# One step of a rational activation: its constant is added on ScalarE and its multiply done on GpSimd for all batches, not for the first alone

## The chip, the cores and the metric

The kernel runs on one core of a Trainium2 chip. The core has TensorE (PE, matrix products), VectorE (DVE), ScalarE (ACT), GpSimd (POOL) and SyncE (SP, which issues the DMAs). The metric is the device time of one execution in microseconds.

## The reference

Attention with a threshold feeds two expert layers, one after the other. There are 4 batches, 8 heads, 576 positions and a head size of 64; the model width is 512 and the hidden width 2048.

```python
scores = scale * q @ k.T
thresh = max(scores) - tau
scores = where(scores >= thresh, scores, -1e9)
attn = exp(scores - max(scores)); attn = attn / (sum(attn) + 1e-9)
x = attn @ v                                  # rows x 512

h = x @ w_in                                  # first expert
P = a[0] + a[1]*h + a[2]*h*h + a[3]*h*h*h
Q = 1.0 + abs(b[0])*abs(h) + abs(b[1])*h*h
x = (P / (Q + 1e-6)) @ w_out

h = x @ w2_in                                 # second expert
g = where(h >= 1, h, where(h <= -1, 0, (h + 1)**2 / 4))
out = g @ w2_out
```

The change is in how `P / (Q + 1e-6)` is worked out.

## The kernel before, in words

Every matrix product of the experts is made of three products of 16-bit halves: a tensor is split into a high half (a cast on ScalarE, L203) and the rest (a subtraction on GpSimd, L207).

The experts are worked through in 192 steps: for each batch, first the first expert (m = 0), then the second (m = 1); for each of these, three blocks j of 192 positions; for each block, eight chunks i of 256 hidden units. A step is one `first_product`: 24 matmuls (L838) into a PSUM bank `ph` (two banks, taken in turn), the activation, and the split of its result into `gg` (four buffers). The `second_product` of a step (24 matmuls, L852, into the accumulator `acc`) is issued three steps later (`LAG = 3`), behind the first product of that later step. At the end of a block `end_moe1` copies `acc` to `y` (ScalarE, L795), takes its largest value (VectorE, L797; over all partitions with a matmul and L183) and splits it (L209, L210).

The activation of the first expert is `rational`. On ScalarE: u = |h| (L719), s = the upper part of the polynomial (L720). On VectorE: u becomes the denominator without its constant (L721), and s the polynomial (L722, L723, both read the PSUM bank). ScalarE estimates 1/Q with Ln and Exp (L724, L725) into r. VectorE finishes the numerator times the estimate (L726). Then comes one Newton step: u = (u + constant) * r, and the result (u - 2) * s (L732). The first half of the Newton step has two forms, chosen by `first`: in batch 0 ScalarE adds the constant (L728) and GpSimd multiplies by r (L729); in batches 1 to 3 one VectorE instruction does both (L731). u and r are the halves of one buffer (tag `tp`, 5 buffers), s has the tag `poly` (3 buffers). The second expert's `quadratic` has one ScalarE and two VectorE instructions (L783 to L785).

The attention of batch 0 comes first, with the preparation of the first expert's weights; the second expert's weights are prepared beside steps 0 to 20 (the casts to words of L223 to L225, the splits of L207). The attention of batches 1, 2 and 3 is spread over steps 18 to 50, 60 to 100 and 108 to 147. A row of it: scores on TensorE (L373, L374), a copy with the maximum on VectorE (L419), the threshold's constants (L420, L421), the exponential on ScalarE (L380), the mask on VectorE (L381), the split (ScalarE L389, GpSimd L390 and L392), a transposing DMA (`eT<-hl`) and the product with v (L407). Before the rows, v and the pairs of q and k are scaled and split (L210, L296, L303, L328).

The order of the instructions on each engine isn't written out by hand. The program gives each step and each attention unit a place (`at(...)`), and a planner that simulates the engines with its own costs (`schedule_with_timeline_sim`) orders each engine's queue by these places and by what it expects to be ready. The queues then run in order on the chip.

Of the kernel before, what the change touches and what calls it, by code (L numbers as in the profile page):

```python
# [12 lines left out]
AF = mybir.ActivationFunctionType  # L13
ALU = mybir.AluOpType
# [25 lines left out]
def tile_attention_moe_moe2(  # L40
# [18 lines left out]
    V, A, G, T, Q = nc.vector, nc.scalar, nc.gpsimd, nc.tensor, nc.sync  # L59
# [43 lines left out]
    def small(n, name, keep=False):  # L103
        if keep:
            return cp.tile([P, n], F32, name=name)
        tag = "".join(x for x in name if x.isalpha() or x == "_").rstrip("_")
        return sp.tile([P, n], F32, name=name, tag=f"s{n}_{tag}", bufs=4 if tag in ("mx", "nt") else 2)
# [30 lines left out]
    qc, pc = small(2, "qc", True), small(4, "pc", True)  # L138
# [61 lines left out]
    def split(hi, lo, src, scale=None, on_vector=True):  # L200

        if scale is None:
            A.copy(hi, src)  # L203

            n = E // 4 if tuple(src.shape) == (P, E) else None
            for p in [slice(c, c + n) for c in range(0, E, n)] if n else [slice(None)]:
                G.tensor_tensor(lo[:, p], src[:, p], hi[:, p], op=ALU.subtract)  # L207
        elif on_vector:
            A.activation(hi, src, AF.Copy, scale=scale)  # L209
            V.scalar_tensor_tensor(lo, src, scale, hi, op0=ALU.mult, op1=ALU.subtract)  # L210
        else:
            A.activation(src, src, AF.Copy, scale=scale)  # L212
            split(hi, lo, src)
# [492 lines left out]
    def temp(name):  # L706

        t = mp.tile([P, 2, W], F32, name=name, tag="tp", bufs=N_TEMP)
        return t[:, 0], t[:, 1]

    def rational(ph, i, consts, name, first):

        sc, ka = consts[0], consts[1][:, i, :]
        p = ph.rearrange("p f t -> p (f t)")
        u, r = temp("t0" + name)
        s = mp.tile([P, W], F32, name="t1" + name, tag="poly", bufs=N_POLY)
        A.activation(u, p, AF.Abs, scale=sc[:, i : i + 1])  # L719
        A.activation(s, p, AF.Identity, bias=ka[:, 2:3], scale=ka[:, 3:4])  # L720
        V.scalar_tensor_tensor(u, u, qc[:, 0:1], u, op0=ALU.add, op1=ALU.mult)  # L721
        V.tensor_tensor(s, s, p, op=ALU.mult)  # L722
        V.scalar_tensor_tensor(s, s, ka[:, 1:2], p, op0=ALU.add, op1=ALU.mult)  # L723
        A.activation(r, u, AF.Ln, bias=lc[:, 1:2], scale=lc[:, 0:1])  # L724
        A.activation(r, r, AF.Exp, bias=lc[:, 2:3], scale=-1.0)  # L725
        V.scalar_tensor_tensor(s, s, ka[:, 0:1], r, op0=ALU.add, op1=ALU.mult)  # L726
        if first:
            A.activation(u, u, AF.Identity, bias=qc[:, 1:2])  # L728
            G.tensor_tensor(u, u, r, op=ALU.mult)  # L729
        else:  # L730
            V.scalar_tensor_tensor(u, u, qc[:, 1:2], r, op0=ALU.add, op1=ALU.mult)  # L731
        V.scalar_tensor_tensor(u, u, 2.0, s, op0=ALU.subtract, op1=ALU.mult)  # L732
        return u

# [42 lines left out]
    def quadratic(ph, i, consts, name):  # L777


        top, bias, su, sg, _ = (x[:, i : i + 1] if e < 4 else x for e, x in enumerate(consts))  # L780
        p = ph.rearrange("p f t -> p (f t)")
        u, g = temp("t2" + name)
        A.activation(u, p, AF.Relu, bias=bias, scale=su)  # L783
        V.scalar_tensor_tensor(u, u, top, u, op0=ALU.min, op1=ALU.mult)  # L784
        V.scalar_tensor_tensor(g, p, sg, u, op0=ALU.mult, op1=ALU.max)  # L785
        return g
# [39 lines left out]
    def first_product(m, b, j, i, consts):  # L826
        name = f"{m}_{b}_{j}_{i}"
        w = chunks[m, i][:, 0:HALF].rearrange("p (x kt f) -> p x kt f", x=2, kt=KT)
        ph = ps_1.tile([P, 512], F32, name="ph" + name, tag=f"ph{i % 2}")[:, 0:W].rearrange("p (f t) -> p f t", f=NF)
        for f in range(NF):  # L830
            n = 0
            for kt in range(KT):
                for wx, xx in ((0, 0), (0, 1), (1, 0)):
                    if m == 0:
                        rhs = xT[b][j][:, xx * KT + kt, :]
                    else:
                        rhs = yT[b, j][:, xx * KT + kt, :]
                    last = T.matmul(ph[:, f, :], w[:, wx, kt, f * P : (f + 1) * P], rhs, start=(n == 0), stop=(n == 3 * KT - 1))  # L838
                    n += 1
        g = rational(ph, i, consts, name, b == 0) if m == 0 else quadratic(ph, i, consts, name)  # L840
        gg = mp.tile([P, 2, NF, TB], F16, name="gg" + name, tag="gg", bufs=N_GG)
        hi, lo = (gg[:, x].rearrange("p f t -> p (f t)") for x in range(2))
        split(hi, lo, g)
        return gg, last.ins
# [19 lines left out]
    for n in range(N_FIRST):  # L864
        with at(36 * n / N_FIRST - 40):
            next(att)
        while halves and len(halves) * N_FIRST > 2 * NCH * (N_FIRST - 1 - n):
            with at(2.4 * (2 * NCH - len(halves)) - 40):
                i, x = halves.pop(0)
# [14 lines left out]
    pending, consts, accs, atts = [], {}, {}, {}  # L884
# [14 lines left out]
    for st, (n, m, b, j, i) in enumerate(steps):  # L899
        with at(st):  # L900
            if i == 0:
                if m == 0:
                    consts[m, b, j] = moe1_consts(b) if j == 0 else consts[m, b, 0]
                else:
                    if b == 0 and j == 0:
                        moe2_weights()
                    consts[m, b, j] = moe2_consts(b, j)
            gg, last = first_product(m, b, j, i, consts[m, b, j])
        pending.append((n, m, b, j, i, gg, last))
        if len(pending) > LAG:  # L910
            with at(st + 1.5):
                finish_step()
        for t, u in beside[st]:
            if u[0] == "w":
                with at(t - 3):
                    stage_half(1, u[1], u[2], False)
            else:
                if u[1] not in atts:
                    atts[u[1]] = attention(u[1])
                with at(t - 1.5):  # L920
                    next(atts[u[1]])
# [31 lines left out]
```

## Time and profile before

| | |
|---|---|
| median of 3 runs | 1272.82 us (1270.37, 1272.82, 1278.93) |
| the profiled execution | 1280.63 us, its span 1278.9 us |
| TensorE busy | 1080.8 us, 85% of the span |
| VectorE busy | 1015.8 us, 79% |
| ScalarE busy | 832.4 us, 65% |
| GpSimd busy | 537.6 us, 42% |

The span goes from the first to the last instruction of the profiled execution. A busy share is the mean over the whole span; the stages differ. Steps of the first expert run in about 214 to 357 us (batch 0), 531 to 655 us (batch 1), 795 to 915 us (batch 2) and 1066 to 1168 us (batch 3). Engines overlap, so busy times don't add up to the span.

### The profile page before, as it was taken

The numbers are of one execution on the slowest core, as the hardware profiler recorded it, in microseconds if no ns is written. First come the engines' busy times: TensorE is split into PE (matmuls) and PEld (weight loads), VectorE is DVE, ScalarE is ACT, GpSimd is POOL, SyncE is SP. The second block draws the span as 40 slices with busy tenths as digits, with TensorE's granted clock in tenths as the row PEclk, the third lists the DMA queues.
The fourth block names the chain that finished last, engine by engine and source line by source line (L and its number), as shares of the span: only waits on it lengthen the run. The fifth ranks groups of instructions, "written<-read, shape, count | busy, mean of one in ns | idle before, by whom it ended". The sixth has DMA issues, their size and how long they took to land.

```text
span 1278.9 us, 31212 instructions
## 1 busy us (share of the span) xinstructions
PE 1080.8 (85%) x12354; PEld 973.4 (76%) x12354; DVE 1015.8 (79%) x2379; ACT 832.4 (65%) x1501; POOL 537.6 (42%) x700
## 2 busy tenths in 40 slices
PE   2667874777837999899889999998898998999998
PEld 1344543767737888899788898997798887999997
DVE  6877879899979987779999666889997767897421
ACT  3656676877865776667776566776765666775332
POOL 3314243877744765421355454212454553222221
PEclk9888987888968999999999999999999999999999
DMA  7745446323665766923398448522783568106100
GB/s 212 236 142 178 148 164 215 116 100 123 228 252 156 130 121 122 251 105 88 72 235 177 92 86 207 172 52 55 185 214 65 106 138 226 39 2 231 35 14 26
DMA packets 220340, 176.37 MB, mean 138 GB/s; under 512 B 182048, under 2 KB 193312, under 8 KB 212000
## 3 DMA queue, kind: packets, MB, share of 16 engines
q1 hardware_dynamic: 220192, 174.36, 50.9%
q8 instruction: 97, 1.59, 0.5%
q14 instruction: 51, 0.42, 0.1%
HBM read 106.83 MB, written 21.50 MB: 100 GB/s over the span
## 4 chain that ended last, share of the span: by engine, by line
PE 35%; DVE 26%; DMA 12%; ACT 9%; issue 8%; POOL 7%; SPq 2%; DVEq 0%; POOLq 0%; ACTq 0%
PE ph L838 14%; PE acc L852 14%; DMA eT<-hl 7%; POOL hl L392 3%; DMA qkT<-qk 2%; PE pv L407 2%; DVE e L381 2%; DMA rqk<-in_k_dram 2%; DVE wt L224 2%; DVE sc L419 2%; DVE t L726 2%; ACT wt L212 1%; POOL wh L207 1%; DVE wt L225 1%; POOL wc L207 1%
## 5 line engine op out<-in xcount | busy, mean ns | idle before, releaser
L852 PE MATMUL acc<-gg,wc 128*128 128x192 f16 x4608 | 434.3, 249 | 28.3 <-POOL gg L207 12.7
L838 PEld LDWEIGHTS <-wc 128*128 128x128 f16 x4608 | 392.2, 100 | 45.3 <-issue 20.4
L852 PEld LDWEIGHTS <-wc 128*128 128x128 f16 x4608 | 389.0, 99 | 25.7 <-issue 19.8
L207 POOL TENSOR_TENSOR gg<-t,gg 128x384 f16<-128x384 f32 x192 | 191.0, 996 | 380.3 <-ACT gg L203 312.9
L838 PE MATMUL ph<-xT,wc 128*128 128x192 f16 x2304 | 219.8, 253 | 28.3 <-DVE t L723 13.8
L838 PE MATMUL ph<-yT,wc 128*128 128x192 f16 x2304 | 219.8, 249 | 1.8 <-DVE t L723 1.4
L392 POOL TENSOR_TENSOR hl<-e,hl 128x256 f16<-128x256 f32 x216 | 156.6, 745 | 0.0
L203 ACT CAST gg<-t 128x384 f16<-128x384 f32 x192 | 97.2, 508 | 82.9 <-DVE t L785 41.0
L784 DVE SCALAR_TENSOR_TENSOR t<-t,c 128x384 f32<-128x384 f32 x96 | 66.3, 691 | 69.5 <-ACT t L783 69.1
L381 DVE SCALAR_TENSOR_TENSOR e<-sc,nt,e 128x576 f32<-128x576 f32 x108 | 96.9, 897 | 28.6 <-ACT e L380 28.1
L390 POOL TENSOR_TENSOR hl<-e,hl 128x64 f16<-128x64 f32 x108 | 41.5, 384 | 149.0 <-ACT hl L389 147.9
L380 ACT ACTIVATE e<-sc,nt,con 128x576 f32<-128x576 f32 x108 | 93.5, 866 | 11.5 <-POOL hl L392 4.9
L407 PE MATMUL pv<-v,eT 128*128 128x65 f16 (+3 forms) x1680 | 70.9, 196 | 33.0 <-DMA eT<-hl 31.5
L783 ACT ACTIVATE t<-ph,c 128x384 f32<-128x384 f32 x96 | 63.8, 666 | 50.8 <-PE ph L838 46.3
L389 ACT CAST hl<-e 128x576 f16<-128x576 f32 x108 | 72.0, 668 | 36.8 <-DVE e L381 34.7
L407 PEld LDWEIGHTS <-eT 128*128 128x128 f16 (+1 forms) x1680 | 64.0, 102 | 41.4 <-DMA eT<-hl 38.8
L719 ACT ACTIVATE t<-ph,sc 128x384 f32<-128x384 f32 x96 | 55.3, 576 | 61.1 <-PE ph L838 60.7
L419 DVE TENSOR_SCALAR_CACHE_REDUCE sc<-s 128x576 f32<-128x576 f32 x108 | 80.8, 749 | 13.2 <-PE s L374 12.5
L207 POOL TENSOR_TENSOR wc<-wt,wc 128x256 f16<-128x256 f32 x64 | 52.1, 847 | 79.6 <-ACT wc L203 79.6
L726 DVE SCALAR_TENSOR_TENSOR t<-t,ka,t 128x384 f32<-128x384 f32 x96 | 68.9, 717 | 14.4 <-ACT t L725 14.2
L724 ACT ACTIVATE t<-t,lc 128x384 f32<-128x384 f32 x96 | 67.8, 707 | 14.7 <-DVE t L721 14.3
L373 PE MATMUL s<-qkT 128*128 128x512 f16 (+1 forms) x240 | 63.8, 294 | 14.3 <-DVE sc L419 7.1
(231 smaller groups left out, 1867.8 us busy)
## 6 DMA issues: line engine op xcount, KB each, us to landing
wc<-scratch SPq DMA_DIRECT2D x56, 1024.0 KB, 5.8
rw<-in_moe_w_in_dram SPq DMA_DIRECT2D x16, 1024.0 KB, 5.3
rw<-in_moe_w_out_dram SPq DMA_DIRECT2D x16, 1024.0 KB, 4.9
scratch<-wc SPq DMA_DIRECT2D x8, 1024.0 KB, 4.3
scratch<-wh SPq DMA_DIRECT2D x16, 512.0 KB, 3.3
rqk<-in_q_dram SPq DMA_DIRECT2D x16, 256.0 KB, 3.0
rqk<-in_k_dram SPq DMA_DIRECT2D x16, 256.0 KB, 3.0
kT<-qkT SPq DMA_DIRECT2D x28, 144.0 KB, 2.4
```

Of the source, the lines that this page charges most:

```text
L203: A.copy(hi, src)
L207: G.tensor_tensor(lo[:, p], src[:, p], hi[:, p], op=ALU.subtract)
L380: A.activation(e, s, AF.Exp, bias=nb, scale=con[:, 0:1])
L381: V.scalar_tensor_tensor(e, s, th, e, op0=ALU.is_ge, op1=ALU.mult)
L389: A.copy(hi, e)
L392: G.tensor_tensor(lo_w[:, p], e[:, whole][:, p], hi[:, whole][:, p], op=ALU.subtract)
L407: T.matmul(pv[rows, 0:w], eT[:, c, cols], vv[:, h * NT + x if x < NT else H * NT + h, at : at + w], start=(n == 0), stop=(n == len(blocks) ...
L419: V.tensor_scalar(s, banks[:, 0:S], 1.0, -LARGEST, op0=ALU.mult, op1=ALU.max, accum_out=mx)
L724: A.activation(r, u, AF.Ln, bias=lc[:, 1:2], scale=lc[:, 0:1])
L726: V.scalar_tensor_tensor(s, s, ka[:, 0:1], r, op0=ALU.add, op1=ALU.mult)
L838: last = T.matmul(ph[:, f, :], w[:, wx, kt, f * P : (f + 1) * P], rhs, start=(n == 0), stop=(n == 3 * KT - 1))
L852: T.matmul(dst, w[:, wx, f, d * P : (d + 1) * P], gg[:, gx, f, :], start=(i == 0 and f == 0 and n == 0 and d % 2 == 0), stop=(i == NCH - 1 ...
```

## The change

The argument `first` of `rational` goes, and with it the second form: in all four batches ScalarE adds the constant and GpSimd multiplies by the estimate. The 72 steps of batches 1 to 3 lose one VectorE instruction each and gain one on ScalarE and one on GpSimd; batch 0 has the same instructions as before.

```diff
-    def rational(ph, i, consts, name, first):
+    def rational(ph, i, consts, name):
...
         V.scalar_tensor_tensor(s, s, ka[:, 0:1], r, op0=ALU.add, op1=ALU.mult)
-        if first:
-            A.activation(u, u, AF.Identity, bias=qc[:, 1:2])
-            G.tensor_tensor(u, u, r, op=ALU.mult)
-        else:
-            V.scalar_tensor_tensor(u, u, qc[:, 1:2], r, op0=ALU.add, op1=ALU.mult)
+        A.activation(u, u, AF.Identity, bias=qc[:, 1:2])
+        G.tensor_tensor(u, u, r, op=ALU.mult)
         V.scalar_tensor_tensor(u, u, 2.0, s, op0=ALU.subtract, op1=ALU.mult)
...
-        g = rational(ph, i, consts, name, b == 0) if m == 0 else quadratic(ph, i, consts, name)
+        g = rational(ph, i, consts, name) if m == 0 else quadratic(ph, i, consts, name)
```

## Rows read from the trace of the kernel before

**Rows 1.** The page's busy times: us, share of the span, instructions.
```profile
PE 1080.8 (85%) x12354; PEld 973.4 (76%) x12354; DVE 1015.8 (79%) x2379; ACT 832.4 (65%) x1501; POOL 537.6 (42%) x700
```

**Rows 2.** Busy by stretch: PE, PEld, DVE, ACT, POOL; clock, DMA share, GB/s.
```profile
214.00:357.00 143.00, 112.70 (x1172) 107.14 (x1172) 130.99 (x219) 111.91 (x193) 98.22 (x88) 0.91 0.46 156
575.00:655.00 80.00, 70.08 (x808) 65.45 (x806) 78.99 (x196) 59.67 (x107) 23.94 (x31) 0.98 0.44 113
840.00:915.00 75.00, 64.16 (x738) 59.76 (x737) 72.37 (x182) 54.46 (x98) 21.54 (x27) 0.98 0.39 97
1066.00:1168.00 102.00, 99.52 (x1231) 98.51 (x1229) 91.61 (x201) 74.62 (x138) 24.88 (x29) 1.00 0.28 90
```

**Rows 3.** TensorE's waits, 575 to 655 us: us in total, times, longest.
```profile
PE ph L838 <- DVE t L723: 3.7, 4, 1.8
...
PE acc L852 <- POOL gg L207: 0.2, 1, 0.2
```

**Rows 4.** TensorE's waits, 840 to 915 us.
```profile
PE s L373 <- DVE sc L419: 4.6, 2, 3.0
PE ph L838 <- DVE t L723: 3.3, 3, 2.1
```

**Rows 5.** Timeline of one step: start us, us, instruction, idle before and its releaser.
```profile
562.70 0.62 DVE L726 SCALAR_TENSOR_TENSOR t<-t,ka,t 128x384 f32<-128x384 f32 x1 [0.45 <-ACT t L725]
563.23 0.61 DVE L731 SCALAR_TENSOR_TENSOR t<-t,qc 128x384 f32<-128x384 f32 x1
...
563.83 0.58 ACT L719 ACTIVATE t<-ph,sc 128x384 f32<-128x384 f32 x1 [1.17 <-PE ph L838]
563.88 0.56 DVE L732 SCALAR_TENSOR_TENSOR t<-t,t 128x384 f32<-128x384 f32 x1
...
565.50 0.92 POOL L207 TENSOR_TENSOR gg<-t,gg 128x384 f16<-128x384 f32 x1 [3.04 <-ACT gg L203]
...
571.49 2.15 PE L852 MATMUL acc<-gg,wc 128*128 128x192 f16 x24
```

**Rows 6.** The Newton step's lines: ns min/median/max, first and last start.
```profile
L728 ACT ACTIVATE t<-t,qc x24: 598/602/627, 219.3 to 352.5; 128x384 f32<-128x384 f32 x24
...
L729 POOL TENSOR_TENSOR t<-t x24: 997/1313/2127, 219.9 to 353.3; 128x384 f32<-128x384 f32 x24
...
L731 DVE SCALAR_TENSOR_TENSOR t<-t,qc x72: 596/611/1262, 536.9 to 1168.8; 128x384 f32<-128x384 f32 x72
```

**Rows 7.** VectorE's groups, 214 to 357 us: busy us, mean ns, idle before.
```profile
L726 DVE SCALAR_TENSOR_TENSOR t<-t,ka,t 128x384 f32<-128x384 f32 x24 | 21.3, 887 | 2.4 <-ACT t L725 2.4
L721 DVE SCALAR_TENSOR_TENSOR t<-t,qc 128x384 f32<-128x384 f32 x24 | 21.1, 879 | 4.3 <-ACT t L719 4.2
L732 DVE SCALAR_TENSOR_TENSOR t<-t,t 128x384 f32<-128x384 f32 x24 | 16.4, 683 | 1.2 <-POOL t L729 1.2
...
L723 DVE SCALAR_TENSOR_TENSOR t<-t,ka,ph 128x384 f32<-128x384 f32 x24 | 14.5, 602 | 0.1
```

**Rows 8.** VectorE's groups, 575 to 655 us.
```profile
L731 DVE SCALAR_TENSOR_TENSOR t<-t,qc 128x384 f32<-128x384 f32 x13 | 8.3, 641 | 0.0
```

**Rows 9.** VectorE's groups, 840 to 915 us.
```profile
L731 DVE SCALAR_TENSOR_TENSOR t<-t,qc 128x384 f32<-128x384 f32 x13 | 8.1, 624 | 0.0
```

**Rows 10.** VectorE's groups, 1090 to 1114 us (batch 3).
```profile
L721 DVE SCALAR_TENSOR_TENSOR t<-t,qc 128x384 f32<-128x384 f32 x6 | 3.7, 618 | 0.5 <-ACT t L719 0.4
L726 DVE SCALAR_TENSOR_TENSOR t<-t,ka,t 128x384 f32<-128x384 f32 x6 | 3.7, 618 | 2.8 <-ACT t L725 2.7
...
L732 DVE SCALAR_TENSOR_TENSOR t<-t,t 128x384 f32<-128x384 f32 x6 | 3.3, 558 | 0.2
```

**Rows 11.** TensorE's waits, 214 to 357 us (batch 0).
```profile
PE acc L852 <- POOL gg L207: 8.9, 4, 3.0
...
PE acc L852 <- ACT gg L203: 6.2, 1, 6.2
```

**Rows 12.** TensorE's waits, whole span.
```profile
PE acc L852 <- DVE mye L183: 7.5, 8, 3.4
```

## The prediction

> **What bounds the kernel now.** I read the table of busy times first. TensorE is busy for 85% of the span and VectorE for 79%, ScalarE and GpSimd far less [rows 1]. No engine bounds the whole, so the next view is the busy time by stretch, for the places where the 72 changed steps run (first expert, batches 1 to 3, 24 steps each) and for batch 0, which already has the new form [rows 2]. Two kinds of stretch show. In 1066 to 1168 us (batch 3) TensorE is busy for 99.52 of 102 us: there it is the bound. In 575 to 655 us (end of batch 1's phase, with the preparation and the first rows of batch 2's attention beside it) VectorE is busy 78.99 of 80 us and TensorE only 70.08; in 840 to 915 us (the same place in batch 2's phase) 72.37 of 75 us against 64.16. There VectorE is the bound. The waits of TensorE agree: in these two stretches its longest ones are for VectorE, for L723, which is the last to read the first product's PSUM bank, and in the second also for L419, which empties a score bank [rows 3, 4]. Batch 3 has next to no such stretch, because no fourth attention follows.
>
> The timeline of one undisturbed step shows what slack there is [rows 5]. VectorE waits 0.45 us for L725 once per step, ScalarE 1.17 us for the next product. The result gg of the step is complete at 565.50 + 0.92 = 566.42 us, and the second product that reads it (three steps later, by the kernel's lag) starts at 571.49: 5.1 us of slack.
>
> **The change part by part.** VectorE loses 72 instructions of L731, 0.61 us each by the median [rows 6]; 13 of them lie in each saturated stretch, 8.3 and 8.1 us of busy time [rows 8, 9]. VectorE's instructions overlap at their ends, so what one takes from the queue is start to start: L726 to L731 is 563.23 - 562.70 = 0.53 us [rows 5]. Removed where it counts: 26 x 0.53 = 13.8 us. The other 46 lie where TensorE is the bound; I cost their removal at nothing, since VectorE already has 0.45 us of idle time in such a step.
>
> ScalarE gains 72 activations of 0.60 us [rows 6]. In a TensorE-bound step they fit into the 1.17 us that it waits. In the saturated stretches it goes from 59.67 to 59.67 + 13 x 0.60 = 67.5 of 80 us and from 54.46 to 62.3 of 75 us: cheap, taken at 0, but if the cover goes (both engines busy together, each waiting in order for the other) it costs at most the same 26 x 0.60 = 15.6 us. Behind the new activation in ScalarE's queue stand the cast of an earlier step (L203), the next step's L719 and the attention row's exponential and cast.
>
> GpSimd gains 72 multiplies: 0.997 us at the least, 1.313 by the median in batch 0 [rows 6], 31.0/24 = 1.29 us by the mean. It has the room: 23.94 + 13 x 1.29 = 40.7 of 80 us. Behind the multiply wait the gg subtraction of an earlier step and the subtractions of attention rows (L390, L392). VectorE's L732 now waits for the multiply. In the plain step L726, which waited for L725, starts at 562.70 [rows 5]; from there L728 takes 0.60 and the multiply 1.0 to 1.3 us, so L732 starts at about 564.3 to 564.6 instead of 563.88: gg is 0.4 to 0.7 us later, against 5.1 us of slack. Cost 0. No DMA and no buffer count changes; three buffers for s and five pairs for u and r each outlive a step by far.
>
> **What the multiply costs VectorE.** In batch 0, L721, L726 and L732 take 0.879, 0.887 and 0.683 us by the mean, and L723, one of whose operands lies in PSUM, 0.602 [rows 7]. In a stretch with little on GpSimd (TensorE-bound, batch 3) the three take 0.618, 0.618 and 0.558 [rows 10]. So GpSimd's work stretches just those VectorE operations that read two tensors of SBUF, by 0.261 + 0.269 + 0.125 = 0.655 us per step of batch 0. GpSimd is busy there for 98.22/24 = 4.09 us per step, most of it weight conversion, so 0.16 us of stretch for each us of GpSimd. For 1.29 us of multiply that is an estimate of 0.21 us per step. Its bounds: nothing (the multiply may meet only L722 and L723), and 0.997 us, the whole shortest multiply, if a VectorE operation stands through it. I take 0.21, the mean of the rows with the same instruction in the same place.
>
> The Trainium skill, page SBUF — State Buffer, section Who interferes with whom, says that a VectorE instruction with two SBUF inputs and a GpSimd instruction that reads SBUF exclude each other for a whole instruction, and one with a single SBUF input does not contend. The rows agree in which lines stretch; by the rule at its worst every multiply blocks for all its length and the sum turns into a loss, the second rival below.
>
> **The sum.** Net of the stretch VectorE gets back 26 x (0.53 - 0.21) = 8.3 us in the saturated stretches. Not all can reach the end. TensorE's share in batch 3's stretch is 99.52/102 = 0.976; the saturated ones can shrink at most until it has that again: 80 - 70.08/0.976 = 8.2 and 75 - 64.16/0.976 = 9.3 us, 17.5 in all. As TensorE is at 88 and 86% there already, and ScalarE rises to 84%, I let three quarters through: 6.2 us. What VectorE gives back stays given back: after these stretches TensorE is the bound, and its queue moves forward as a whole. The 7.5 us in which TensorE waits for the maximum at the end of a product (L183) [rows 12] can shrink or grow, as one instruction fewer stands before it on VectorE and one more before its ScalarE copy: taken at 0, bounds -3.8 and +3.8 (half of it). The planner orders the instructions anew by its own costs from the changed steps on; what that gives I can't see and take at 0. The profiled execution took 1280.63 us (span 1278.9), 7.8 above the median of the runs. 1280.63 - 6.2 = 1274.4, and by the same distance 1272.82 - 6.2 = **1266.6 us**, 0.5% faster.
>
> **The rivals.** First, all of the 13.8 us reaches the end, because the multiply falls beside operations it doesn't disturb, and shorter waits at the ends of products come on top: 13.8 to 17.5 us, 1255 to 1259 us. For it: VectorE is without a gap in 575 to 655 us, so each instruction less counts. Against: batch 0's stretched rows.
>
> Second, the slower one: GpSimd holds VectorE up. Place: the two saturated stretches. If a two-operand VectorE operation stands through each multiply, VectorE loses 26 x (0.997 - 0.53) = 12.1 us, 1285 us; and once VectorE is later than now, gg is late too: in batch 0 TensorE waited 8.9 us for gg on GpSimd and 6.2 for its cast in 24 steps [rows 11], at which rate 26 steps cost 16.4 us, 1289 us. It decides from 0.53 us of stretch per multiply on. For it: 0.655 us per step in batch 0. Against: batch 0 has 4.1 us of GpSimd work per step, these stretches would have 40.7/14 = 2.9, and TensorE waits there for gg on GpSimd 0.2 us in all [rows 3]. That two-operand rule of the page named above is what this rival would be.
>
> Third, the change does to the time nothing that can be seen: VectorE's freed slots are filled with waiting for the multiply and for the attention's transposes, while TensorE's idle time stays. 1270 to 1275 us. For it: a chain through four engines in order gains little from relieving one.
>
> **How the numbers follow.** My forecast gets 0.40, the first rival 0.24, the slower one 0.18, no effect 0.18. One per cent (12.7 us) is about what a measurement of this kernel can tell from no change. Faster by more than that: the first rival and a little of the forecast's own spread, 0.26. Slower by more: most of the second, 0.16. Within: 0.58. The range goes from 1255 less the 3.8 us at the ends of products, 1252 in round numbers, up to 1287, between the two prices of the slower rival; about 2 in 10 is left outside. The forecast's own range is 1260 to 1272.
>
> **What would show it.** Right: the profile up to the first changed step (about 530 us) as now; in the phases of batches 1 to 3 VectorE below 97% busy in the stretches that answer to 575 to 655 and 840 to 915, these shorter by 2 to 5 us each, TensorE's waits for L723 and L419 shorter; L721, L726 and L732 up by some 0.2 us per step together; L729 near 1.0 to 1.3 us. Wrong: VectorE still without gaps there with these lines stretched by over 0.5 us per step, waits of TensorE for gg of over 5 us, attention's transposes later than now, or a gap where the planner has moved other work.

## The result and the profile after

The changed kernel takes 1287.44 us (median of 4 runs, 1285.45 to 1289.85) against 1274.49 us of the kernel before in the same hour: a ratio of 1.0104 (95% interval 1.0074 to 1.0134), 13 us slower. Measured twice more beside other kernels it was 1.0106 (1.0068 to 1.0144) and 1.0111 (1.0076 to 1.0146). The forecast was 0.5% faster.

In the file after, L728 and L729 of before are L727 and L728, and what stands behind them has moved up by three: L732 is L729, L795 and L797 are L792 and L794, the products L838 and L852 are L835 and L849. The busy times, which answer to [rows 1]:

```profile
PE 1086.2 (84%) x12354; PEld 974.4 (76%) x12354; DVE 1005.3 (78%) x2307; ACT 865.5 (67%) x1573; POOL 618.5 (48%) x772
```

VectorE lost 72 instructions of 0.64 us, 46 us if they are simply added up, and is only 10.5 us less busy. The stretches, chosen to answer to those of [rows 2] (the same order of columns):

```profile
580.00:661.00 81.00, 70.05 (x814) 65.48 (x812) 78.87 (x185) 65.34 (x121) 40.62 (x43) 0.98 0.46 110
845.00:920.00 75.00, 63.87 (x711) 60.31 (x710) 73.58 (x172) 61.04 (x112) 38.89 (x41) 0.93 0.30 73
1075.00:1178.00 103.00, 98.75 (x1217) 97.38 (x1216) 85.73 (x172) 86.12 (x161) 49.27 (x52) 1.00 0.26 86
```

In the first two VectorE is as full as before (97 and 98%) and TensorE as idle. In batch 3 TensorE's share has fallen from 97.6 to 95.9%. (The granted clock of 0.93 in the second stretch is taken up under what stays open.)

VectorE's groups of the step from batch 1 on (530 us to the end), first before, then after (busy us, mean ns, idle time before and what ended it):

```profile
L726 DVE SCALAR_TENSOR_TENSOR t<-t,ka,t 128x384 f32<-128x384 f32 x72 | 47.6, 661 | 12.0 <-ACT t L725 11.8
L731 DVE SCALAR_TENSOR_TENSOR t<-t,qc 128x384 f32<-128x384 f32 x72 | 45.9, 637 | 0.0
L721 DVE SCALAR_TENSOR_TENSOR t<-t,qc 128x384 f32<-128x384 f32 x72 | 45.2, 627 | 5.0 <-ACT t L719 4.5
...
L723 DVE SCALAR_TENSOR_TENSOR t<-t,ka,ph 128x384 f32<-128x384 f32 x72 | 43.8, 609 | 1.1
L732 DVE SCALAR_TENSOR_TENSOR t<-t,t 128x384 f32<-128x384 f32 x72 | 42.0, 583 | 1.0
```

```profile
L726 DVE SCALAR_TENSOR_TENSOR t<-t,ka,t 128x384 f32<-128x384 f32 x72 | 56.1, 781 | 9.6 <-ACT t L725 8.4
L721 DVE SCALAR_TENSOR_TENSOR t<-t,qc 128x384 f32<-128x384 f32 x72 | 53.3, 740 | 7.1 <-ACT t L719 6.8
...
L729 DVE SCALAR_TENSOR_TENSOR t<-t,t 128x384 f32<-128x384 f32 x72 | 46.0, 638 | 18.9 <-POOL t L728 18.8
...
L723 DVE SCALAR_TENSOR_TENSOR t<-t,ka,ph 128x384 f32<-128x384 f32 x72 | 43.7, 608 | 1.1
```

The three operations that read two tensors of SBUF are longer by 0.120, 0.113 and 0.055 us; L723, with an operand in PSUM, is not (as in [rows 7]). And VectorE now stands still for 18.8 us until the multiply is done. In the timeline one can watch the first effect. Two steps of batch 3 after, a plain one and one at the end of a block (columns as in [rows 5]):

```profile
1148.11 1.00 POOL L728 TENSOR_TENSOR t<-t 128x384 f32<-128x384 f32 x1 [0.96 <-ACT t L727]
...
1148.53 0.99 DVE L721 SCALAR_TENSOR_TENSOR t<-t,qc 128x384 f32<-128x384 f32 x1 [0.35 <-ACT t L719]
1149.44 0.55 DVE L729 SCALAR_TENSOR_TENSOR t<-t,t 128x384 f32<-128x384 f32 x1
1149.56 0.71 ACT L724 ACTIVATE t<-t,lc 128x384 f32<-128x384 f32 x1 [0.50 <-DVE t L721]
...
1160.37 1.27 POOL L728 TENSOR_TENSOR t<-t 128x384 f32<-128x384 f32 x1 [0.80 <-ACT t L727]
...
1160.80 1.26 DVE L721 SCALAR_TENSOR_TENSOR t<-t,qc 128x384 f32<-128x384 f32 x1
...
1162.92 0.60 DVE L723 SCALAR_TENSOR_TENSOR t<-t,ka,ph 128x384 f32<-128x384 f32 x1
...
1163.58 1.91 PE L835 MATMUL ph<-xT,wc 128*128 128x192 f16 x21 [2.10 <-DVE t L723]
```

L721 starts while the multiply runs and ends 0.41 us after it (1149.52 against 1149.11), not 0.61 us after its own start: it stood until GpSimd was done. ScalarE's Ln (L724) waits for it. In a plain step TensorE doesn't notice. At the end of a block, where the copy and the maximum of y come on top, the same thing makes L723 late, and TensorE waits 2.10 us. (In the last sixteen steps of batch 3 it waits 4.0 us for L723, at the ends of two blocks; before it waited there 1.0 us, for L183.) Its waits for L723 from batch 1 on, before and after:

```profile
PE ph L838 <- DVE t L723: 7.3, 8, 2.1
```

```profile
PE ph L835 <- DVE t L723: 13.8, 11, 3.4
```

ScalarE's idle time that I had counted on is gone as well; its longest waits in batch 3's stretch (1066 to 1168 us before, 1075 to 1178 us after):

```profile
ACT t L719 <- PE ph L838: 23.5, 19, 4.2
ACT t L724 <- DVE t L721: 2.1, 4, 1.0
ACT gg L203 <- DVE t L732: 1.4, 4, 0.5
```

```profile
ACT t L724 <- DVE t L721: 6.1, 13, 0.8
ACT gg L203 <- DVE rk_s L156: 4.0, 2, 2.0
ACT gg L203 <- DVE t L729: 4.0, 6, 1.1
ACT t L719 <- PE ph L835: 3.6, 4, 2.4
```

So after the first profile there were three suspects: GpSimd holding VectorE up, ScalarE being full, and the longer ring of waits (ScalarE, GpSimd, VectorE, ScalarE, each in order). All queues have the same order as before up to the first changed step; behind it the planner has ordered them anew.

### The profile page after: what moved, and what is told of

Same layout as the page of the kernel before. It is cut to its first block, busy times and chain, and to the rows that moved or that the text cites. A ratio compares the mean times of both kernels' runs of the same rounds, so it can differ in the third digit from the quotient of the medians.

```text
span 1287.7 us, 31344 instructions
## 1 busy us (share of the span) xinstructions
PE 1086.2 (84%) x12354; PEld 974.4 (76%) x12354; DVE 1005.3 (78%) x2307; ACT 865.5 (67%) x1573; POOL 618.5 (48%) x772
## 3 DMA queue, kind: packets, MB, share of 16 engines
q1 hardware_dynamic: 220192, 174.36, 50.7%
## 4 chain that ended last, share of the span: by engine, by line
PE 29%; DVE 24%; ACT 13%; DMA 13%; POOL 10%; issue 9%; SPq 2%; DVEq 0%; POOLq 0%; ACTq 0%
PE ph L835 12%; PE acc L849 11%; DMA eT<-hl 7%; POOL hl L392 3%; POOL gg L207 2%; DVE t L726 2%; DVE t L729 2%; DMA qkT<-qk 2%; DVE t L721 2%; DVE e L381 2%; DMA rqk<-in_k_dram 2%; ACT wt L212 1%; PE pv L407 1%; POOL wc L207 1%; ACT hl L389 1%
## 5 line engine op out<-in xcount | busy, mean ns | idle before, releaser
L849 PE MATMUL acc<-gg,wc 128*128 128x192 f16 x4608 | 434.1, 249 | 22.6 <-POOL gg L207 10.2
L835 PEld LDWEIGHTS <-wc 128*128 128x128 f16 x4608 | 393.0, 100 | 52.5 <-issue 23.2
L849 PEld LDWEIGHTS <-wc 128*128 128x128 f16 x4608 | 387.9, 99 | 19.9 <-issue 14.4
L207 POOL TENSOR_TENSOR gg<-t,gg 128x384 f16<-128x384 f32 x192 | 197.3, 1029 | 257.1 <-ACT gg L203 256.5
L835 PE MATMUL ph<-xT,wc 128*128 128x192 f16 x2304 | 221.1, 253 | 37.0 <-DVE t L723 20.8
L835 PE MATMUL ph<-yT,wc 128*128 128x192 f16 x2304 | 220.2, 248 | 1.3 <-DVE rk_f L155 1.0
L728 POOL TENSOR_TENSOR t<-t 128x384 f32<-128x384 f32 x96 | 108.5, 1133 | 105.7 <-ACT t L727 97.0
L726 DVE SCALAR_TENSOR_TENSOR t<-t,ka,t 128x384 f32<-128x384 f32 x96 | 77.3, 806 | 11.9 <-ACT t L725 10.7
L724 ACT ACTIVATE t<-t,lc 128x384 f32<-128x384 f32 x96 | 67.6, 706 | 27.1 <-DVE t L721 26.2
L721 DVE SCALAR_TENSOR_TENSOR t<-t,qc 128x384 f32<-128x384 f32 x96 | 73.9, 770 | 11.3 <-ACT t L719 10.9
```

Source lines behind the costliest of these rows:

```text
L849: T.matmul(dst, w[:, wx, f, d * P : (d + 1) * P], gg[:, gx, f, :], start=(i == 0 and f == 0 and n == 0 and d % 2 == 0), stop=(i == NCH - 1 ...
```

## The experiments

All are edits of the kernel before in the branch for batches 1 to 3, compared with the kernel before on the same chip. Ratio, interval, and VectorE's busy time of the whole profile (before: 1015.8 us):

| kernel | ratio | interval | VectorE us |
|---|---|---|---|
| multiply left out | 0.9934, again 0.9957 | 0.9917 to 0.9951, 0.9929 to 0.9984 | 982.6, 981.8 |
| wait without reading | 0.9967 | 0.9941 to 0.9993 | 975.1 |
| GpSimd writes only | 1.0011 | 0.9988 to 1.0035 | 1014.8 |
| ScalarE adds, VectorE multiplies | 1.0017 | 1.0002 to 1.0031 | 1019.6 |
| change in batch 3 only | 1.0025 | 0.9998 to 1.0052 | 1010.9 |
| change in batches 1 and 2 only | 1.0059 | 1.0034 to 1.0085 | 1007.1 |
| ScalarE load nobody waits for | 1.0073 | 1.0053 to 1.0092 | 1018.4 |
| multiply nobody waits for | 1.0080 | 1.0055 to 1.0105 | 1018.9 |
| the change | 1.0104, 1.0106, 1.0111 | see above | 1005.3 |
| VectorE adds, GpSimd multiplies | 1.0125 | 1.0104 to 1.0145 | 1026.4 |
| GpSimd load nobody waits for | 1.0184 | 1.0158 to 1.0209 | 1044.9 |

### One half of the change at a time

```diff
-            V.scalar_tensor_tensor(u, u, qc[:, 1:2], r, op0=ALU.add, op1=ALU.mult)
+            A.activation(u, u, AF.Identity, bias=qc[:, 1:2])
+            V.tensor_tensor(u, u, r, op=ALU.mult)
```

> Batches 1 to 3: ScalarE adds the constant, VectorE multiplies (a two-tensor multiply in the place of the fused one); GpSimd gets nothing. Three theories for the 13 us that the change cost. GPSIMD HOLDS VECTORE (the multiply on GpSimd stretches VectorE's two-tensor operations, and so the saturated stretches stay as long): this kernel within 0.3% of the kernel before, VectorE's L721 and L726 at their old means (0.65, 0.68 us). SCALARE FULL (0.6 us more per step takes the idle time that absorbed disturbances): 0.7 to 1.3% slower than before, as the change. RING (the step now passes ScalarE, GpSimd, VectorE and ScalarE again, each in order, so that a cast waits on ScalarE for GpSimd and holds the next step's Ln): half of the change's loss, 0.3 to 0.7% slower, because one link is there and the longest one (GpSimd) is not.

0.17% slower: with ScalarE's whole new load on the step's path the loss is 2 us. The plain multiply takes VectorE 0.569 us where the fused one took 0.637; L721 and L726 take 0.633 and 0.677, near the 0.627 and 0.661 of before.

```diff
-            V.scalar_tensor_tensor(u, u, qc[:, 1:2], r, op0=ALU.add, op1=ALU.mult)
+            V.tensor_scalar(u, u, qc[:, 1:2], None, op0=ALU.add)
+            G.tensor_tensor(u, u, r, op=ALU.mult)
```

> Batches 1 to 3: VectorE adds the constant (one tensor, one scalar), GpSimd multiplies; ScalarE gets nothing. GPSIMD HOLDS VECTORE: slower than the change itself or like it, 1.0 to 1.6% slower than before, since VectorE keeps an instruction and has GpSimd's multiply beside it. SCALARE FULL: within 0.4% of before. RING: 0.4 to 1.0% slower than before, the GpSimd link is there, ScalarE's queue is shorter by one.

1.25% slower, though ScalarE has nothing more to do than before. The loss goes with GpSimd's half.

### Load that nobody waits for

```diff
             V.scalar_tensor_tensor(u, u, qc[:, 1:2], r, op0=ALU.add, op1=ALU.mult)
+            G.tensor_tensor(r, r, r, op=ALU.mult)
```

> The kernel before with one multiply more on GpSimd per step of batches 1 to 3, of r by itself after its last reader; nothing reads it. (The output is that of before.) GPSIMD HOLDS VECTORE: 0.8 to 1.5% slower, as the 72 multiplies stretch VectorE in the saturated stretches and no instruction was taken from it. SCALARE FULL: no difference over 0.3%. RING: no difference over 0.4%, since nothing waits for the multiply; only its place in GpSimd's queue ahead of gg.

1.84% slower, 23 us, more than the theory of holding gave it and far more than the ring's. Nothing on the step's path was added; VectorE's busy time grew by 29.1 us, 0.40 us for each of the 72 multiplies, and L721 went from 627 to 891 ns:

```profile
L721 DVE SCALAR_TENSOR_TENSOR t<-t,qc 128x384 f32<-128x384 f32 x72 | 64.1, 891 | 2.9 <-ACT t L719 2.5
```

```diff
             V.scalar_tensor_tensor(u, u, qc[:, 1:2], r, op0=ALU.add, op1=ALU.mult)
+            A.activation(r, r, AF.Identity, bias=qc[:, 1:2])
```

> The kernel before with one activation more on ScalarE per step of batches 1 to 3, of r after its last reader; nothing reads it. SCALARE FULL: 0.7 to 1.3% slower, ScalarE's wait for TensorE's product in batch 3 falls from 23 us to under 8. GPSIMD HOLDS VECTORE: no difference over 0.3%. RING: 0 to 0.4% slower, the activation stands in ScalarE's queue and nothing comes back to it.

0.73% slower, which looks like a full ScalarE, though its wait for TensorE's product in batch 3 fell to 11 us and not under 8. But the half of the change with as much on ScalarE lost 0.17%, and the kernel with the multiply left out (below), with the same ScalarE load and 72 VectorE instructions fewer, is faster than before. What differs is that this activation waits in ScalarE's queue for VectorE's last reader of r, and what stands behind waits with it:

```profile
ACT t L732 <- DVE t L731: 7.6, 9, 3.3
...
ACT t L732 <- DVE t L726: 6.3, 8, 1.7
```

That these 13.9 us are its loss was not tried by itself.

### Reading or writing

```diff
             V.scalar_tensor_tensor(u, u, qc[:, 1:2], r, op0=ALU.add, op1=ALU.mult)
+            G.memset(r, 0.0)
+            G.memset(r, 0.0)
```

> As the run with GpSimd's idle multiply, but in its place two memsets of r after its last reader: GpSimd writes and reads nothing, nobody reads the result. That run was 1.84% slower, VectorE's busy time from batch 1 on 600.8 us against 571.4. HOLD BY READING (a GpSimd instruction that reads SBUF stands against VectorE's second tensor): within 0.4% of before, VectorE's busy time under 577 us, L731 and L721 at their old means. GPSIMD'S QUEUE OR THE NEW ORDER (gg and the attention's subtractions behind one more instruction, all queues ordered anew): over 1% slower again if the memsets take as long as the multiply, less in proportion if they are shorter.

Within 0.1% of before. GpSimd had 60 us more to do, at the place of the idle multiply and with gg behind it in the queue, and the planner ordered the queues anew; VectorE's busy time is that of before, and L721 takes 0.647 us. That speaks against GpSimd's queue and the new order as such, and for the reading. (Of VectorE's 2307 other instructions some 200 stand elsewhere in its queue than before in the run with the idle multiply, some 280 here, some 500 in the change.) The memsets:

```profile
L733 POOL MEMSET t<- 128x384 f32 x72 | 30.2, 419 | 3.8
L732 POOL MEMSET t<- 128x384 f32 x72 | 30.1, 418 | 105.6 <-DVE t L731 64.3 <-DVE t L726 10.0 <-DVE nt L421 5.2
```

The Trainium skill, page SBUF — State Buffer, section Who interferes with whom, states just this difference: VectorE's second tensor stands against a GpSimd instruction that reads SBUF, not against one that only writes it. The two runs agree with it. That an instruction with a single SBUF input goes free, as the prediction cites it, the same section of the Trainium skill says of those outside VectorE's two-port modes; no run here tells the modes apart.

### Where

```diff
-        g = rational(ph, i, consts, name, b == 0) if m == 0 else quadratic(ph, i, consts, name)
+        g = rational(ph, i, consts, name, b in (0, 3)) if m == 0 else quadratic(ph, i, consts, name)
```

> The new form in batch 3 (and batch 0, as before) only; batches 1 and 2 keep the fused VectorE instruction. In the profiles so far the last two blocks of batch 3's first expert, where TensorE was busy 98% of the time, take 32.6 and 32.6 us before, 34.3 and 34.9 with the change, 35.8 and 36.4 with GpSimd's idle multiply. HOLD (GpSimd's multiply stretches VectorE's two-tensor operations also where TensorE is the bound, and uses up VectorE's slack there): 0.2 to 0.5% slower than before, these blocks above 34 us each. SATURATED STRETCHES ONLY (the loss arises beside the attention): within 0.2% of before.

0.25% slower, 3.2 us, at the edge of its interval (from 0.3 us faster to 6.6 us slower). The last 16 steps of batch 3's first expert, from the first activation to the last, before and here:

```profile
L719 ACT ACTIVATE t<-ph,sc x16: 568/580/583, 1103.7 to 1164.9; 128x384 f32<-128x384 f32 x16
```

```profile
L719 ACT ACTIVATE t<-ph,sc x16: 559/562/581, 1093.2 to 1158.8; 128x384 f32<-128x384 f32 x16
```

61.2 us became 65.6. They are 65.6 in the change too, 67.6 with the idle multiply, 61.3 with the memsets.

In these sixteen steps the order of the queues is no rival: before, with the memsets and with the idle multiply each engine has the same instructions in the same order, but for the added ones. L721 in them, before (1103.6 to 1168 us), with the memsets (1096.6 to 1161 us) and with the idle multiply (1112.6 to 1183.5 us):

```profile
L721 DVE SCALAR_TENSOR_TENSOR t<-t,qc 128x384 f32<-128x384 f32 x16 | 10.5, 657 | 0.0
```

```profile
L721 DVE SCALAR_TENSOR_TENSOR t<-t,qc 128x384 f32<-128x384 f32 x16 | 10.4, 651 | 0.0
```

```profile
L721 DVE SCALAR_TENSOR_TENSOR t<-t,qc 128x384 f32<-128x384 f32 x16 | 17.0, 1064 | 0.1
```

The granted clock is 1.00 before and with the memsets, 0.97 with the idle multiply; the first eight of its steps, ahead of the fall, take 35.8 us against 32.6.

```diff
-        g = rational(ph, i, consts, name, b == 0) if m == 0 else quadratic(ph, i, consts, name)
+        g = rational(ph, i, consts, name, b < 3) if m == 0 else quadratic(ph, i, consts, name)
```

> The new form in batches 0, 1 and 2; batch 3 keeps the fused VectorE instruction. HOLD: the rest of the change's loss, 0.5 to 0.9% slower than before, batch 3's blocks back at 32.6 us. SATURATED STRETCHES ONLY: the whole loss, 0.9 to 1.3%. If the sum of this run's and the batch 3 run's loss is far from the change's, the order of the queues, made anew each time, matters more than the place.

0.59% slower, and batch 3's last sixteen steps are back at 61.2 us. The two parts make 0.84% of the change's 1.06% in the same hour, inside the intervals. By these ratios batch 3, where TensorE is the bound, carries a quarter to a third of the loss; its interval alone reaches from none to half.

> The changed kernel again, on the same chip and beside the same runs of the kernel before as the three others: 0.8 to 1.3% slower than before by every theory. It is there so that the parts are compared with the whole of the same hour.

1.06% slower.

### The multiply left out, the wait left out, the wait alone

In these three the Newton step is incomplete: the first two leave the multiply by r out, the third sets u to zero in its place.

```diff
-            V.scalar_tensor_tensor(u, u, qc[:, 1:2], r, op0=ALU.add, op1=ALU.mult)
+            A.activation(u, u, AF.Identity, bias=qc[:, 1:2], scale=2.0**-12)
```

> Batches 1 to 3: ScalarE adds the constant (scaled down, so that the values stay in range), and the multiply by the estimate is left out, on every engine; the output is not that of the reference. VectorE loses its 72 instructions, GpSimd gains nothing. This is what the prediction's step on VectorE's freed time is worth by itself, with nothing taken back. PREDICTION'S STEP: 26 x 0.53 = 13.8 us fewer in the saturated stretches, three quarters to all of it at the end: 0.8 to 1.1% faster than before. If SCALARE or the order of the queues takes it all: within 0.3%.

0.66% faster, 8.4 us (6.2 to 10.6), and 0.43% in the second run. Less than the expected 0.8%, but the term is there: VectorE's freed time reaches the end when nothing takes it back.

```diff
-            V.scalar_tensor_tensor(u, u, qc[:, 1:2], r, op0=ALU.add, op1=ALU.mult)
+            A.activation(u, u, AF.Identity, bias=qc[:, 1:2], scale=2.0**-12)
+            G.tensor_tensor(r, r, r, op=ALU.mult)
```

> As the run with the multiply left out, but GpSimd multiplies r by itself after its last reader, and nobody waits for it. VectorE loses 72 instructions, ScalarE and GpSimd have the change's load; only the wait of VectorE's last instruction for GpSimd is missing (the output is not the reference's). HOLD alone (the stretch of VectorE's two-tensor operations, some 0.4 to 0.5 us per multiply, is all of it): as the change, 0.8 to 1.2% slower than before. HOLD AND WAIT: the stretch gives back what the removal brought, within 0.4% of before, and the other 0.6 to 1.0% of the change are the wait through four engines in order. Either way 0.8 to 1.7% slower than the run with the multiply left out.

0.80% slower. Against the run before it, on the same chip, the multiply alone costs 1.0080 - 0.9934 = 1.46%, 18.6 us, and 36.3 us of VectorE's busy time (982.6 to 1018.9). Nothing keeps VectorE's last instruction apart from the multiply here, and it runs into it in 54 of the 72 steps, 1.022 us by the mean instead of 0.601:

```profile
L733 DVE SCALAR_TENSOR_TENSOR t<-t,t 128x384 f32<-128x384 f32 x72 | 73.6, 1022 | 4.9 <-DVE con L332 0.3
```

The change lost 1.04 to 1.11%, so up to 0.3% may be left for the wait beside a multiply; the intervals overlap.

```diff
-            V.scalar_tensor_tensor(u, u, qc[:, 1:2], r, op0=ALU.add, op1=ALU.mult)
+            A.activation(u, u, AF.Identity, bias=qc[:, 1:2])
+            G.memset(u, 0.0)
+            G.memset(u, 0.0)
```

> Batches 1 to 3: ScalarE adds the constant as in the change, and in the place of GpSimd's multiply stand two memsets of u (0.42 us each in the earlier run), for which VectorE's last instruction waits as it waits for the multiply. GpSimd reads nothing there; the multiply is left out, so the output is not the reference's. THE WAIT COSTS BY ITSELF: 0.3 to 0.9% slower than the run with the multiply left out, that is from 0.4% faster than before to 0.2% slower, with VectorE standing still for GpSimd for over 8 us in all. ONLY THE STRETCH COSTS: within 0.25% of the run with the multiply left out, 0.4 to 0.9% faster than before.

0.33% faster than before, 0.10% behind the run with the multiply left out beside it, less than either interval. VectorE stands still for GpSimd as long as in the change, 19.1 us against 18.8:

```profile
L734 DVE SCALAR_TENSOR_TENSOR t<-t,t 128x384 f32<-128x384 f32 x72 | 40.2, 558 | 19.7 <-POOL t L733 19.1
```

By itself the wait costs nothing that can be told from these intervals. Batch 3's last 16 steps take 60.8 us here. (The memsets take 0.84 us together, the multiply about 1.0 to 1.1.)

> The kernel with the multiply left out, again, beside the run with the wait alone: 0.5 to 0.8% faster than before.

0.43% faster (0.16 to 0.71), just under what was expected.

> The changed kernel on the same chip: 0.9 to 1.2% slower than before. What it loses beyond the run with the wait alone is the stretch by GpSimd's reading: 0.8 to 1.5% if the stretch carries most of the loss, under 0.6% if the wait does.

The change lost 1.11% beside them, so what lies between it and the wait alone is 1.0111 - 0.9967 = 1.44%, 18.4 us: the price of a multiply that reads in the place of two memsets, found a second way. It holds all that comes with the multiply, the new order of the queues too.

### Two more

```diff
-        g = rational(ph, i, consts, name, b == 0) if m == 0 else quadratic(ph, i, consts, name)
+        g = rational(ph, i, consts, name, False) if m == 0 else quadratic(ph, i, consts, name)
```

> The opposite edit: batch 0 gets the fused VectorE instruction too, so that no multiply of this step runs on GpSimd anywhere. HOLD: in batch 0 GpSimd is busy 69% of the time with reading instructions anyway; VectorE gets 24 instructions of 0.6 us more and loses 0.4 to 0.65 us of stretch for each: within 0.4% of before, faster rather than slower. If VectorE's instruction count decides (VectorE is 92% busy there): 0.4 to 1.0% slower.

1.0016 (0.9997 to 1.0035), no difference. In batch 0, as far as the interval tells, the trade of a VectorE instruction for a multiply on GpSimd is even, not a gain.

> The kernel before, unchanged, for a second profile of it. The two profiles of the changed kernel reach batch 1's first changed step 4 us later than the one profile of before, though all queues have the same order up to there. By every theory this is the scatter of single executions: batch 1 should begin between 533 and 538 us, and the blocks after it differ by up to 3 us from the first profile.

Batch 1's first activation comes at 537.0 us here and at 533.1 in the first profile; 537.6, 537.2 and 534.8 in three profiles of the change. So the 4 us by which the change's profile seemed late before its first changed step are the scatter of single executions, and no part of the 13 us.

## Why the prediction was wrong

Where the time went shows in the lengths of blocks, from the first activation of a step (L719, or L783 in the second expert) to the first behind the block or blocks, in us; several numbers are several profiles of the same kernel:

| | before | multiply left out | wait alone | GpSimd writes only | the change | idle multiply |
|---|---|---|---|---|---|---|
| batch 1, first expert, blocks 2 and 3 | 89.3, 89.2 | 85.2, 85.2 | 86.0 | 90.2 | 88.6, 88.7, 88.7 | 93.4 |
| batch 2, first expert, blocks 2 and 3 | 89.6, 89.5 | 85.2, 85.6 | 83.1 | 90.0 | 90.3, 90.4, 90.9 | 94.5 |
| batch 3, first expert, all blocks | 100.9, 99.4 | 98.8, 98.7 | 99.0 | 99.4 | 104.0, 105.2, 104.0 | 107.3 |
| batch 2, second expert, block 1 | 45.9, 43.5 | 47.0, 47.1 | 45.7 | 44.8 | 50.7, 51.1, 52.7 | 46.3 |

The first two rows hold the saturated stretches of the prediction (26 of their 32 steps).

- **The bound, and what VectorE's instructions are worth: right, a little high.** With 13.8 us freed in the saturated stretches and three quarters of it let through, the step gives 10.4 us. The multiply left out gained 8.4 and, again, 5.5, and by the first two rows 8.2 us in just these blocks. That removing L731 is worth next to nothing in a step where TensorE is the bound was right too: batch 3's last sixteen steps took 61.2 us with it and 61.1 without.
- **What the multiply costs VectorE: the step that failed.** It was put at 0.21 us per multiply and at 26 of the 72 multiplies, 4.1 us at the end after the same three quarters. The whole price measured 18.6 and 18.4 us. Its size was wrong: in the first two rows alone the change is 8.6 us behind the multiply left out, 0.27 us for each of their 32 steps, where 0.21 by three quarters makes 0.16. VectorE's busy time over all steps, 982.6 us without the multiply and 1005.3 with it, gives 0.32 us each in the change, 0.40 and 0.50 in the other two runs. It had been scaled from batch 0 by GpSimd's busy time, as if GpSimd met VectorE at random; in the change 40 of the 72 multiplies lie beside an L721, L726 or L729 of over 0.7 us. And it had counted the step's three lines alone: in batch 2's two blocks the step's VectorE instructions add up to 50.1 us with the multiply left out and 51.6 with the change, but the 129 and 128 others (attention, splits, weights) to 45.1 and 51.2. Its place was wrong as well:
- **The 46 steps outside these stretches, where a multiply was costed at nothing: wrong.** The cover was VectorE's 0.45 us and ScalarE's 1.17 us per plain step. It holds in the plain step of batch 3. It was needed at the ends of blocks, where L795's copy and L797's maximum come on top. Batch 3's first expert takes 4 us more than before in the table; the run with batch 3 alone lost 3.2 us, with nothing inside its interval.
- **In the saturated stretches: no gain.** Forecast were 6.2 us less in all and 2 to 5 us less in each; the first two rows together became 0.4 us longer, as the 8.2 us that the removal gave there were taken back whole. VectorE stayed at 97 and 98%.
- **The wait for the multiply, ScalarE's load, GpSimd's queue: right at nothing or near it.** The wait alone cost 0.10%, ScalarE's half 0.17%, TensorE's wait for gg on GpSimd went from 12.7 to 10.2 us over the span.
- **The slower rival gave the time (1285 to 1289 us) by half of the right mechanism.** GpSimd does hold VectorE up, as the section of the Trainium skill's page SBUF — State Buffer cited there has it. But gg was not late, and its point of decision, 0.53 us per multiply in the saturated stretches, was too high: the removal brought only 8.2 us there, 0.26 us for each of the 32 steps, and a price of 0.27 us ate that. The rest of the loss lies outside these stretches, where the rival, like the forecast, had put none; that its time came out is in part luck.

What stays open: VectorE is 10.5 us less busy in the change than before, and the kernel is slower; and the run with ScalarE's half and the run with the multiply that nobody waits for have the same VectorE and ScalarE busy times within 4 us and differ by 0.63%. So the sum alone doesn't decide; when in the step VectorE is held may, and the order of the queues differs too. In TensorE-bound blocks the path is seen (L723). In batch 2 the trace puts 5 to 7 us into the second expert's first block (43.5 and 45.9 us in two profiles of before, 50.7 to 52.7 in four profiles with the change there), which has no changed instruction. That is up to half of the loss. The idle multiply, which lost more, has none of it (46.3). The planner moved more of batch 3's attention into this block (18 or 19 matmuls of L373 instead of 12), but the wait alone has 18 there too and takes 45.7 us; it was not taken apart.

The clock is open as well. From batch 1's start TensorE spends 20 to 24 us at the lower of its two levels (1.2 GHz) in three profiles of the change, 20 and 7 in two of before, 3 to 7 with the multiply left out or the wait alone; its matmuls of 192 columns follow each other at 160 ns there and at 82 ns at the higher level. By the mean granted clock of all executions (0.939 and 0.942 for the change, 0.943 and 0.944 for before beside it) the change has an estimated 6 to 11 us more at the lower level, worth at most 3 to 6 of its 13 us. Whether that follows from TensorE's longer waits no run shows.

## What to carry to other kernels

Before work is moved from VectorE to GpSimd, look at what both read: a GpSimd instruction that reads SBUF took back 0.3 to 0.5 us per instruction of 1 us from VectorE operations with two tensors in SBUF, where the move freed 0.46 (33.2 us in 72 steps). Price it on every instruction moved and for all that VectorE does beside it, in stretches with another bound too: what fits into a plain step need not fit at the end of a block. To find out which of load, wait and contention costs, put the load where nobody waits, then replace it by one that only writes, then keep the wait alone.

## What the runs showed that was not expected

- Two memsets on GpSimd per step (60 us in all) left VectorE's busy time where it was (1014.8 against 1015.8 us); 77.8 us of multiplies at the same place added 29.1 us.
- 19 us of VectorE standing still in its queue for GpSimd cost 0.1% of the time, less than the intervals can tell; with the multiply, which waits as long and stretches VectorE by 0.3 us per step, it was 1.4% more.
- One more activation on ScalarE cost 0.17% where it followed ScalarE's own work and 0.73% where it waited for VectorE, for the same 0.6 us. (In the first of the two VectorE's instruction was another one as well.)
- Even an instruction of one number per partition can stand until GpSimd is done. L685, 0.15 us before, took 0.95 us once in the change and ended with the multiply (608.39 and 608.38 us):

```profile
607.08 1.30 POOL L728 TENSOR_TENSOR t<-t 128x384 f32<-128x384 f32 x1
...
607.44 0.95 DVE L685 TENSOR_TENSOR mb<-hb,mb 128x1 f32<-128x1 f32 x1
```
